# A fused attention and mixture-of-experts kernel: the rank matmuls one step later, the zero-and-one rows in blocks, and two moves in the first expert passes

## The chip, the cores and the metric

The kernel runs on one core of a Trainium2 chip. The metric is the device time of one execution in microseconds. Every kernel is run several times; the profile is one further execution that was recorded instruction by instruction, so its own time need not be the median of the others.

## The reference: what is computed

Attention over 8 batches x 8 heads, 576 positions, 64 wide, where each position sees itself and the 63 before it. Its output, as 4608 rows of 512, goes to a top-1 mixture of 8 experts:

```
mask = (rel >= 0) & (rel < 64)                # rel = query position - key position
attn = softmax(where(mask, q k^T / 8, -1e9))
x = (attn v), as 4608 rows x 512
logits = x @ w_gate                           # 512 x 8
e = argmax(logits); g = softmax(logits)[e]
out[row] = g * (relu(x[row] @ w1[e]) @ w2[e]) # w1 512 x 1024, w2 1024 x 512
```

All in float32, within a tolerance that the kernel keeps by splitting each float32 factor into a rounded part and its remainder (hi and lo) and adding three products.

## The kernel before, in words

**Attention steps.** The rows are cut into 36 tiles of 128. The main loop (L781) is a software pipeline of 43 steps; step i works on several tiles at once: the scores of tile i (TensorE, L368), their masking and maximum (VectorE: L379, L385, L387), the exponentials of tile i-1 (ScalarE, L395), the copy `tsb` of the transposed probabilities of tile i-2 (ScalarE, L404) and their masked halves `pm` (GpSimd, L411, two instructions), the product with the values for tile i-3 (TensorE, L425), its normalisation `xrow` (VectorE, L431 to L435), and, for tile i-4, the transpose of the finished rows (L442) and a copy (ScalarE, L449). The finished rows go to a table `xs` in memory.

**Routing.** Logits are made for two tiles at a time in two steps (L487 and L488, then L469 and L472). The tiles form four rounds of 8, 6, 12 and 10 (`ROUNDS`). When a round's logits are complete, `route` puts eight pieces s1 to s8 into the queue `slow`, and step by step they are taken out. Pieces s1 to s3 (VectorE) find the expert of each token as a 0/1 row `oh`; s4 (TensorE, L521 and L523, then a ScalarE copy `rks`, L525) counts each token's rank among those of its expert; s5 to s8 (VectorE, a little GpSimd) turn ranks into positions. s4 is marked: it is run at the start of a step, the others at a step's end, three per step (`RATE[0]`). Then the queue `puts` is emptied, three entries per step (`RATE[1]`; four from step 36 on): `put(t)` (L570) writes one 128x128 block `hot_row[:, t]` that has a one where a token's position equals the column. After rounds 1 and 2 two more entries follow: `early_parts` (L579, L583, L586: small products `here` and `said`) and one that books for the next three steps the matmuls that make a small table of row numbers (`early_table`, L593, read at L598 to L606), and two gathers (`early_rows`, L170) that fetch the rows of two experts from `xs` into `xg`. The gather for expert 0 fills `xg[0]` with two instructions, which lines 805 and 806 turn (L181, copied by L183 and L184 to `xeh` and `xel`) in steps 27 and 28.

**First passes.** From step 29 on, four early passes (one per expert 0 to 3, 256 rows each, `first_passes`) are woven between the pieces of the attention steps, and go on after the loop. A pass has eight slices j: 12 matmuls with w1 (L286), relu (ScalarE `hh` L292, VectorE `hl` L293), and the matmuls with w2 of the slice before (L250). Each slice of weights is split by ScalarE (`whi`, L224, or L228 ahead of time) and VectorE (`wlo`, L221). After the slices j = 4 and 5 of a pass, the two blocks of rows of the next early pass are turned. `split_ahead` keeps one slice split ahead inside the loop; behind the loop a slice is split where `expert` asks for it (L277). There, between the pieces of the passes, `plan` (L649) computes on VectorE which blocks the later passes take; its pieces are taken one every third piece of a pass. `table(0, NMA)` (L593, 36 matmuls) reads out the row numbers of all later passes.

**Order.** Inside the loop and the early passes the program order is written by hand; every engine takes its instructions in that order, whatever is ready. PSUM banks are shared: `t_b` holds the transposed probabilities and, from step 29, the transposed rows and the turned rows; the scores have two banks, from step 29 only one.

Of the kernel before, what the change touches and what calls it, by code (L numbers as in the profile page):

```python
# [24 lines left out]
P = 128  # L25
# [35 lines left out]
LOADW = 14  # L61
RATE = (3, 3)
AHEAD = 2
# [49 lines left out]
def window_attention_then_top1_moe(ctx: ExitStack, tc: tile.TileContext, qkv, wall, wg, cst, out):  # L113
# [376 lines left out]
    def route(nt, lgs, t0, rnd):  # L490
# [61 lines left out]
        def s8():  # L552
# [6 lines left out]
            nc.vector.tensor_tensor(out=val[:, ts_, 3], in0=v["g1"], in1=val[:, ts_, 2], op=ALU.subtract)  # L559
            for t in range(nt):  # L560
                puts.append(lambda t=t: put(t))
            if rnd in SNAP:
                e0, rows = SNAP[rnd], t0 + nt
                puts.append(lambda: early_parts(e0, rows))
                puts.append(lambda: begin.extend(
                    (rs_["step"] + 1 + k, f) for k, f in enumerate([lambda: early_table(e0, rows)] + [
                        lambda e=e: early_rows(e, rows) for e in range(e0, e0 + 2)])))

        def put(t):
            nc.vector.tensor_scalar(out=hot_row[:, t0 + t], in0=rowb, scalar1=v["lo"][:, t:t + 1], scalar2=None,  # L570
                                    op0=ALU.is_equal)

        slow.extend((f is s4, f) for f in (s1, s2, s3, s4, s5, s6, s7, s8))

# [33 lines left out]
    def early_parts(e, nt):  # L608
        for b in parts(rt, cc("first")[:, 2 * e:2 * e + 4], nt, 4):
            keep["early"] = b  # L610

# [142 lines left out]
    def first_passes():  # L754
        for e in range(EARLY):
            ms = range(2 * e, 2 * e + 2)
            for j in expert(xe[e % 2], cols(eidx, ms), cols(egate, ms), ew[e],
                            lambda: ew[e + 1] if e + 1 < EARLY else wts[0]):
                if e + 1 < EARLY and j == 3:
                    ew[e + 1] = Weights(e + 1)  # L760
                if e + 1 < EARLY and j in (4, 5):
                    turn(xg[(e + 1) % 3], j - 4, xe[(e + 1) % 2])
                    if (e, j) == (EARLY - 2, 5):
                        keep["turned"] = True
                yield e, j
# [14 lines left out]
    with tc.manual_schedule():  # L780
        for i in range(NS + LAST):  # L781
# [12 lines left out]
            if slow and slow[0][0]:  # L794
                slow.popleft()[1]()
            while begin and begin[0][0] <= i:
# [63 lines left out]
        rest = steps()  # L860
        for e, j in early:
            next(rest, None)
            if e == EARLY - 1 and j == NJ - 3:
# [66 lines left out]
```

## Time and profile before

| | |
|---|---|
| three runs | 686.11, 689.41, 689.62 us (median 689.41) |
| the profiled execution | 684.16 us, span of its instructions 682.4 us |
| TensorE busy | 625.0 us, 92% of the span |
| VectorE busy | 413.8 us, 61% |
| ScalarE busy | 359.5 us, 53% |
| GpSimd busy | 194.9 us, 29% |
| mean granted TensorE clock | 0.981 of full speed |

A busy share is an average over the stages. PE is TensorE, PEld its weight loads, DVE VectorE, ACT ScalarE, POOL GpSimd. In a timeline each row is a start, a duration, the engine, the line of the kernel, the operation, what it writes and reads, how many equal instructions were merged, and in brackets how long the engine had stood idle and what ended the wait.

### The profile page before, as it was taken

Reading aid. Unit: us, or ns where it says so; the run is one execution under the profiler, and the core shown is the slowest. Engines: PE = TensorE matmul, PEld = TensorE weight load, DVE = VectorE, ACT = ScalarE, POOL = GpSimd, SP = SyncE. Lnnn points to the kernel's source line nnn. Section 1 sums busy time; section 2 is a strip of 40 time slices with the busy share of each in tenths; the row PEclk is TensorE's granted clock in tenths of the full one; section 3 lists DMA queues with packets and bytes.
Section 4 is the critical chain, followed back from the end, with each engine's and each line's share of the span. In section 5 each row is a group of like instructions: output and inputs, shape, how many; then the busy total and the mean of one; then the engine's idle time right before and its main releaser. Section 6 shows DMA issues by size and latency. Waiting matters only on the chain.

```text
span 682.4 us, 17092 instructions
## 1 busy us (share of the span) xinstructions
PE 625.0 (92%) x7002; PEld 551.8 (81%) x7002; DVE 413.8 (61%) x805; ACT 359.5 (53%) x760; POOL 194.9 (29%) x171
## 2 busy tenths in 40 slices
PE   5797987887789888999999999999999999999995
PEld 4686776766677677889999999999999999999994
DVE  4775978664865896464444655565655556555651
ACT  4564764654453343553535555555556565555551
POOL 4564654632334113330112122121213121110011
PEclk9998986999999999999999999999999999999998
DMA  8997874772324554864354666666567566555620
GB/s 296 332 286 254 281 250 167 268 239 97 109 95 175 198 172 142 326 207 144 142 168 172 229 220 224 216 222 233 166 238 231 208 222 228 202 206 186 217 93 32
DMA packets 34247, 138.14 MB, mean 202 GB/s; under 512 B 4844, under 2 KB 5996, under 8 KB 24432
## 3 DMA queue, kind: packets, MB, share of 16 engines
q1 hardware_dynamic: 27760, 118.08, 50.2%
q0 software_dynamic: 6400, 18.88, 7.9%
q8 instruction: 57, 0.93, 0.5%
q14 instruction: 30, 0.25, 0.1%
HBM read 119.11 MB, written 19.92 MB: 204 GB/s over the span
## 4 chain that ended last, share of the span: by engine, by line
PE 73%; DVE 13%; issue 6%; ACT 4%; POOL 2%; DMA 1%; POOLq 0%; DVEq 0%; ACTq 0%
PE m_b L286 16%; PE x_b L250 14%; PE s_b L250 14%; PE t_b L286 13%; PE x_b L425 5%; PE s_b L368 3%; ACT pf L395 2%; PE s_b L181 2%; DVE wlo L221 2%; DVE xrow L435 1%; PE x_b L487 1%; POOL pm L411 1%; DVE s_b L385 1%; DMA ring<-qkv 1%; DVE s_b L379 1%
## 5 line engine op out<-in xcount | busy, mean ns | idle before, releaser
L221 DVE TENSOR_TENSOR wlo<-raw,whi 128x1024 fp32r<-128x1024 f32 (+1 forms) x158 | 187.2, 1185 | 167.1 <-ACT whi L224 163.0
L224 ACT CAST whi<-raw 128x1024 fp32r<-128x1024 f32 (+1 forms) x147 | 149.1, 1015 | 102.1 <-PE s_b L250 51.3
L411 POOL TENSOR_TENSOR pm<-tsb,cs 128x512 f32<-128x512 f32 x72 | 91.2, 1288 | 93.5 <-ACT tsb L404 85.2
L258 POOL DMA_INDIRECT out<-ys,idx_sb x32 | 40.9, 1277 | 182.9 <-ACT ys L257 178.0
L170 POOL DMA_INDIRECT xg<-xs,idx_sb x32 | 34.3, 1072 | 156.5 <-PE s_b L181 139.1
L286 PE MATMUL t_b<-xh,whi 128*128 128x256 f32 (+1 forms) x240 | 70.6, 294 | 0.0
L286 PE MATMUL m_b<-xh,whi 128*128 128x256 f32 (+1 forms) x240 | 70.5, 294 | 0.0
L250 PE MATMUL s_b<-whi,hh 128*128 128x512 f32 x176 | 70.4, 400 | 0.0
L286 PE MATMUL m_b<-xh,wlo 128*128 128x256 f32 (+1 forms) x240 | 69.9, 291 | 0.0
L250 PE MATMUL s_b<-whi,hl 128*128 128x512 f32 x176 | 69.3, 394 | 0.6 <-DVE hl L293 0.6
L286 PE MATMUL m_b<-xl,whi 128*128 128x256 f32 (+1 forms) x240 | 69.7, 290 | 0.2 <-DVE xl L184 0.2
L395 ACT ACTIVATE pf<-s_b,mxs 128x64 f32<-128x64 f32 x288 | 62.9, 336 | 12.9 <-PE s_b L368 6.7
L286 PE MATMUL t_b<-xh,wlo 128*128 128x256 f32 (+1 forms) x240 | 69.6, 290 | 0.0
L250 PE MATMUL s_b<-wlo,hh 128*128 128x512 f32 x176 | 69.5, 395 | 0.0
L286 PE MATMUL t_b<-xl,whi 128*128 128x256 f32 (+1 forms) x240 | 69.2, 288 | 0.0
L292 ACT ACTIVATE hh<-m_b 128x256 fp32r<-128x256 f32 (+1 forms) x82 | 32.5, 396 | 59.6 <-PE m_b L286 59.5
L425 PE MATMUL x_b<-ring,pm 64*64 64x65 f32 x2176 | 49.0, 233 | 14.4 <-issue 4.8
L425 PEld LDWEIGHTS x_b<-ring,pm 64*64 64x64 f32 x2176 | 43.8, 145 | 19.9 <-issue 15.4
L250 PE MATMUL x_b<-wlo,hh 128*128 128x512 f32 x144 | 56.7, 394 | 0.0
L250 PE MATMUL x_b<-whi,hl 128*128 128x512 f32 x144 | 56.5, 393 | 0.0
L250 PE MATMUL x_b<-whi,hh 128*128 128x512 f32 x144 | 56.5, 392 | 0.0
L293 DVE SCALAR_TENSOR_TENSOR hl<-m_b,hh 128x256 fp32r<-128x256 f32 (+1 forms) x82 | 35.4, 432 | 25.0 <-ACT hh L292 24.9
(178 smaller groups left out, 1280.0 us busy)
## 6 DMA issues: line engine op xcount, KB each, us to landing
raw<-wall SPq DMA_DIRECT2D x76, 1024.0 KB, 4.9
ring<-qkv SPq DMA_DIRECT2D x66, 386.0 KB, 4.6
xs<-xrow SPq DMA_DIRECT2D x36, 256.0 KB, 2.9
ring<-qkv SPq DMA_DIRECT2D x4, 256.0 KB, 5.6
ring<-qkv SPq DMA_DIRECT2D x4, 130.0 KB, 5.4
ring<-qkv SPq DMA_DIRECT2D x1, 512.0 KB, 3.8
xg<-xs,idx_sb POOLq DMA_INDIRECT x32, 4.1
out<-ys,idx_sb POOLq DMA_INDIRECT x32, 2.8
```

The source lines that it names most:

```text
L170: nc.gpsimd.indirect_dma_start(out=t[:, u], out_offset=None, in_=xs[0:rows], in_offset=bass.IndirectOffsetOnAxis(ap=ix, axis=0), bounds_ch ...
L221: nc.vector.tensor_tensor(out=lo[:, s], in0=raw[:, s], in1=hi[:, s], op=ALU.subtract)
L224: nc.scalar.copy(out=hi[:, s], in_=raw[:, s])
L250: nc.tensor.matmul(y, lhsT=x[:, us], rhs=w[:, C:], start=(j == 0 and m == 0), stop=(j == NJ - 1 and m == 2))
L258: ins = nc.gpsimd.indirect_dma_start(out=out, out_offset=bass.IndirectOffsetOnAxis(ap=ix, axis=0), in_=ys, in_offset=None, bounds_check=N ...
L286: nc.tensor.matmul(hp[:, 0:w], lhsT=a[:, ks], rhs=x[:, kk, 0:w], start=(m == 0), stop=(m == 11))
L292: nc.scalar.activation(out=hh[:, 0:w], in_=hp[:, 0:w], func=AF.Relu)
L293: nc.vector.scalar_tensor_tensor(out=hl[:, 0:w], in0=hp[:, 0:w], scalar=0.0, in1=hh[:, 0:w], op0=ALU.max, op1=ALU.subtract)
L368: nc.tensor.matmul(sp[cols, a, g], lhsT=q_r[rows, r, g], rhs=k_r[rows, r - 1:r + 1, g], start=True, stop=True)
L395: nc.scalar.activation(out=pf[:, g, a], in_=sp[:, a, g, 0], func=AF.Exp, bias=mx[:, h:h + 1], scale=SCALE)
L411: nc.gpsimd.tensor_tensor(out=pm[i], in0=t.rearrange("p (g q) -> p g q", g=NG), op=ALU.mult, in1=cc("mask")[:, i * P:(i + 1) * P].unsqueez ...
L425: nc.tensor.matmul(x_b[cols, a, g * V1:(g + 1) * V1], lhsT=pm[i][rows, g, cols], rhs=v_r[rows, c % RING - i, g], start=(i == 0), stop=(i = ...
```

## The change

Six edits. In `route`, an empty entry that is marked like s4 is put before s4 in all rounds but the last, so that s4 runs a step later. `put` writes up to four blocks with one instruction that compares two broadcast operands, and its queue entries become blocks of four tiles; two entries per step are taken instead of three. `early_parts` becomes three entries of two instructions each. In the early passes the two blocks of the next pass are turned after the slices j = 5 and 6. Behind the loop, `split_ahead` is called, and the VectorE half of the split queued, after each slice, ahead of the next piece of `plan`.

```
-RATE = (3, 3)
+RATE = (3, 2)
+PUT = 4
...
-            for t in range(nt):
-                puts.append(lambda t=t: put(t))
+            for t in range(0, nt, PUT):
+                puts.append(lambda t=t: put(t, min(t + PUT, nt)))
...
-                puts.append(lambda: early_parts(e0, rows))
+                puts.extend(early_parts(e0, rows))
...
-        def put(t):
-            nc.vector.tensor_scalar(out=hot_row[:, t0 + t], in0=rowb, scalar1=v["lo"][:, t:t + 1], scalar2=None,
-                                    op0=ALU.is_equal)
-
-        slow.extend((f is s4, f) for f in (s1, s2, s3, s4, s5, s6, s7, s8))
+        def put(a, b):
+            nc.vector.tensor_tensor(out=hot_row[:, t0 + a:t0 + b], in0=rowb.unsqueeze(1).to_broadcast([P, b - a, P]),
+                                    in1=v["lo"][:, a:b].unsqueeze(2).to_broadcast([P, b - a, P]), op=ALU.is_equal)
+
+
+        again = (None,) if rnd + 1 < len(ROUNDS) else ()
+        slow.extend((f in (None, s4), f) for f in (s1, s2, s3, *again, s4, s5, s6, s7, s8))
...
     def early_parts(e, nt):
-        for b in parts(rt, cc("first")[:, 2 * e:2 * e + 4], nt, 4):
-            keep["early"] = b
+        made = []
+
+        def some(k):
+            if not made:
+                made.append(parts(rt, cc("first")[:, 2 * e:2 * e + 4], nt, 4))
+            for _ in range(k):
+                keep["early"] = next(made[0])
+
+        return [lambda k=k: some(k) for k in (2, 2, 2)]
...
-                if e + 1 < EARLY and j in (4, 5):
-                    turn(xg[(e + 1) % 3], j - 4, xe[(e + 1) % 2])
-                    if (e, j) == (EARLY - 2, 5):
+                if e + 1 < EARLY and j in (5, 6):
+                    turn(xg[(e + 1) % 3], j - 5, xe[(e + 1) % 2])
+                    if (e, j) == (EARLY - 2, 6):
                         keep["turned"] = True
...
             if slow and slow[0][0]:
-                slow.popleft()[1]()
+                f = slow.popleft()[1]
+                if f:
+                    f()
...
         for e, j in early:
+            if j is not None:
+                split_ahead()
+                while lows:
+                    lows.popleft()()
             next(rest, None)
```

What this does to the order is shown at three places. First TensorE at round 1 (6 tiles), where step 19 ends and step 20 begins, before the change: transposes of step 19 (L442, L400), the first of the rank matmuls, then the scores and values of step 20.

```order
L469 MATMUL x_b<-cs_81,lgT 128x128 x2
L442 MATMUL m_b<-cs_81,xrow 128x128 x4
L400 MATMUL t_b<-cs_81,pf 128x128 x4
L521 LDWEIGHTS tri
L521 MATMUL x_b<-oh,tri 128x56
...
L523 MATMUL x_b<-oh,ones 128x8
L368 MATMUL s_b_75<-ring 64x128 x16
L425 MATMUL x_b<-ring,pm_1746 64x65 x4
```

The same place after the change (line numbers one higher); L369 is the scores, L426 the values, L488 the logits, L443 and L401 the transposes of step 20.

```order
L443 MATMUL m_b<-cs_81,xrow 128x128 x4
L401 MATMUL t_b<-cs_81,pf 128x128 x4
L369 MATMUL s_b_75<-ring 64x128 x16
...
L488 MATMUL x_b<-xT,wg_sb 32x128 x8
L443 MATMUL m_b<-cs_81,xrow 128x128 x4
L401 MATMUL t_b<-cs_81,pf 128x128 x4
L522 LDWEIGHTS tri
L522 MATMUL x_b<-oh,tri 128x56
...
L524 MATMUL x_b<-oh,ones 128x8
L369 MATMUL s_b_76<-ring 64x128 x16
```

The scores, values, logits and transposes of step 20 now stand between the transposes of step 19 and the rank matmuls, which stand before the scores of step 21.

Second VectorE after round 1, where the blocks `hot_row` are written, before: the last of s8 (`val`), three blocks, a quarter of a weight split, and the start of the next step's masking.

```order
L558 CAST val<-g_2043 128x6
L559 TENSOR_TENSOR val<-g_2043,val 128x6
L570 TENSOR_SCALAR hot_row<-rowb,lo 128x128 x3
L221 TENSOR_TENSOR wlo<-raw,whi 128x256
L378 MEMSET s_b_75 64x8x64
...
L488 COPY lgT<-x_b 128x256
L570 TENSOR_SCALAR hot_row<-rowb,lo 128x128 x3
```

After:

```order
L559 CAST val<-g_2135 128x6
L560 TENSOR_TENSOR val<-g_2135,val 128x6
L571 TENSOR_TENSOR hot_row<-rowb,lo 128x512
L571 TENSOR_TENSOR hot_row<-rowb,lo 128x256
L222 TENSOR_TENSOR wlo<-raw,whi 128x256
L380 COPY_PREDICATED s_b_76<-fold,s_b_76 128x8x64
```

All six tiles of the round are written in one step by two instructions; the step is step 22, one later than the first three blocks before.

Third GpSimd, where the gathers of experts 0 and 1 (`xg_97` is `xg[0]`, `xg_98` is `xg[1]`) stand between the `pm` pairs of the steps, before:

```order
L411 TENSOR_TENSOR pm_2288<-tsb,cs_81 128x512
L411 TENSOR_TENSOR pm_2289<-tsb,cs_81 128x512
L170 DMA xg_97<-xs,eidx 128x512 x2
L411 TENSOR_TENSOR pm_2391<-tsb,cs_81 128x512
L411 TENSOR_TENSOR pm_2392<-tsb,cs_81 128x512
L170 DMA xg_98<-xs,eidx 128x512 x2
```

After:

```order
L412 TENSOR_TENSOR pm_2253<-tsb,cs_81 128x512
L412 TENSOR_TENSOR pm_2254<-tsb,cs_81 128x512
L412 TENSOR_TENSOR pm_2375<-tsb,cs_81 128x512
L412 TENSOR_TENSOR pm_2376<-tsb,cs_81 128x512
L171 DMA xg_97<-xs,eidx 128x512 x2
L412 TENSOR_TENSOR pm_2464<-tsb,cs_81 128x512
L412 TENSOR_TENSOR pm_2465<-tsb,cs_81 128x512
L171 DMA xg_98<-xs,eidx 128x512 x2
```

Both gathers stand one `pm` pair, that is one step, later (steps 26 and 27 instead of 25 and 26), while the turns of `xg[0]` stay in steps 27 and 28.

## Rows read from the trace of the kernel before

**Rows 1.** The page: the span in 40 equal slices, TensorE's busy tenths and its granted clock.

```profile
PE   5797987887789888999999999999999999999995
...
PEclk9998986999999999999999999999999999999998
```

**Rows 2.** Busy time in four stretches: start and end, length, then for each engine its busy time and instructions, the granted clock, the share of the DMA engines and GB/s.

```profile
60.00:140.00 80.00, 65.82 (x1716) 56.79 (x1718) 61.77 (x183) 47.77 (x174) 44.29 (x41) 0.89 0.71 243
140.00:212.00 72.00, 61.56 (x1185) 50.76 (x1178) 46.16 (x122) 33.55 (x96) 25.16 (x21) 0.98 0.36 124
...
234.00:300.00 66.00, 59.35 (x391) 52.36 (x390) 46.91 (x89) 31.45 (x48) 16.77 (x14) 1.00 0.56 198
300.00:656.00 356.00, 355.82 (x2216) 322.68 (x2215) 197.73 (x257) 195.59 (x289) 64.28 (x54) 1.00 0.59 203
```

**Rows 3.** TensorE's timeline at the rank matmuls of round 0 (first row) and round 1, with the scores and values behind them and the scores of the step after.

```profile
62.34 0.19 PE L521 MATMUL x_b<-oh,tri 128*128 128x72 bf16 x1 [1.76 <-DVE oh L516]
...
89.70 0.19 PE L521 MATMUL x_b<-oh,tri 128*128 128x56 bf16 x1 [2.17 <-DVE oh L516]
...
89.95 1.90 PE L368 MATMUL s_b<-ring 64*64 64x128 f32 x32
91.61 1.98 PE L425 MATMUL x_b<-ring,pm 64*64 64x65 f32 x64
...
95.11 1.10 PE L368 MATMUL s_b<-ring 64*64 64x128 f32 x32
```

**Rows 4.** VectorE's timeline in the same two steps: the instructions before which it stood idle.

```profile
64.67 0.70 DVE L379 COPY_PREDICATED s_b<-fold,s_b 128x512 f32<-128x512 int32 x1 [2.38 <-ACT pf L395]
...
67.00 0.17 DVE L431 TENSOR_SCALAR den<-x_b 128x8 f32<-128x8 f32 x1 [0.70 <-PE x_b L487]
...
91.90 0.70 DVE L379 COPY_PREDICATED s_b<-fold,s_b 128x512 f32<-128x512 int32 x1 [1.91 <-PE s_b L368]
...
94.30 0.17 DVE L431 TENSOR_SCALAR den<-x_b 128x8 f32<-128x8 f32 x1 [0.77 <-PE x_b L487]
```

**Rows 5.** The timeline of VectorE (s8's first instruction in round 0, then two groups of three blocks in round 1) and of GpSimd (the `pm` pair beside the first of these groups).

```profile
72.09 0.69 DVE L553 SCALAR_TENSOR_TENSOR lo<-mid,pf 128x8 f32<-128x8 f32 x1
...
101.03 2.73 DVE L570 TENSOR_SCALAR hot_row<-rowb,lo 128x128 bf16<-128x128 bf16 x3
...
107.70 0.57 DVE L570 TENSOR_SCALAR hot_row<-rowb,lo 128x128 bf16<-128x128 bf16 x3
...
101.19 2.52 POOL L411 TENSOR_TENSOR pm<-tsb,cs 128x512 f32<-128x512 f32 x2 [0.80 <-ACT tsb L404]
```

**Rows 6.** Groups of equal instructions on VectorE: busy time, mean ns of one, idle time before them.

```profile
L435 DVE TENSOR_TENSOR xrow<-x_b,rs 128x512 f32<-128x512 f32 x36 | 24.9, 691 | 1.4 <-DVE rs L433 0.2
L570 DVE TENSOR_SCALAR hot_row<-rowb,lo 128x128 bf16<-128x128 bf16 x36 | 10.4, 348 | 0.0
...
L293 DVE SCALAR_TENSOR_TENSOR hl<-m_b,hh 128x256 fp32r<-128x256 f32 x74 | 31.0, 418 | 22.8 <-ACT hh L292 22.7
```

**Rows 7.** TensorE's timeline in steps 23 and 24: the values of step 23 and the scores of step 24.

```profile
107.92 2.01 PE L425 MATMUL x_b<-ring,pm 64*64 64x65 f32 x64 [3.80 <-DVE lgT L488]
...
113.27 1.98 PE L368 MATMUL s_b<-ring 64*64 64x128 f32 x32
```

**Rows 8.** The gathers: GpSimd's timeline (first gather of expert 0, the `pm` pair of step 25, first gather of expert 1), TensorE's (scores of step 25, then the two turns of `xg[0]`), and the time from issue to landing of the four gathers of line 170 between 100 and 135 us.

```profile
117.19 1.25 POOL L170 DMA_INDIRECT xg<-xs,eidx  x1 [0.17 <-issue]
...
121.49 2.68 POOL L411 TENSOR_TENSOR pm<-tsb,cs 128x512 f32<-128x512 f32 x2 [1.74 <-ACT tsb L404]
124.32 1.04 POOL L170 DMA_INDIRECT xg<-xs,eidx  x1 [0.15 <-issue]
...
118.72 1.10 PE L368 MATMUL s_b<-ring 64*64 64x128 f32 x32
...
127.16 0.66 PE L181 MATMUL m_b<-cs,xg 128*128 128x128 f32 x4 [0.24 <-ACT xT L449]
...
131.83 0.66 PE L181 MATMUL m_b<-cs,xg 128*128 128x128 f32 x4 [0.24 <-ACT xT L449]
...
DMA to landing us min/median/max: 3.5/5.8/6.5
```

**Rows 9.** TensorE's timeline at the rank matmuls of round 2 (step 32) and the scores behind them.

```profile
160.82 0.21 PE L521 MATMUL x_b<-oh,tri 128*128 128x104 bf16 x1 [1.28 <-DVE oh L516]
...
163.34 1.10 PE L368 MATMUL s_b<-ring 64*64 64x128 f32 x32 [1.52 <-ACT pf L395]
```

**Rows 10.** TensorE's timeline in steps 34 and 35: a matmul that waits for split weights, and the row transposes behind the two turns of expert 1's rows.

```profile
182.89 0.38 PE L286 MATMUL m_b<-xeh,wlo 128*128 128x256 f32 x1 [0.79 <-DVE wlo L221]
185.03 0.66 PE L442 MATMUL t_b<-cs,xrow 128*128 128x128 f32 x4 [1.75 <-DVE xel L184]
...
194.68 0.66 PE L442 MATMUL t_b<-cs,xrow 128*128 128x128 f32 x4 [1.40 <-DVE xel L184]
```

**Rows 11.** Behind the loop: TensorE's timeline at a wait for split weights and at the table, and VectorE's at a split after two other pieces of work.

```profile
235.35 0.39 PE L286 MATMUL m_b<-xeh,wlo 128*128 128x256 f32 x1 [0.73 <-DVE wlo L221]
...
261.94 2.65 PE L593 MATMUL s_b<-said,hot_row 128*128 128x160 bf16 x36 [1.40 <-DVE xel L184]
...
246.92 1.35 DVE L583 TENSOR_TENSOR said<-here,val 128x1152 bf16<-128x1152 bf16 x1
249.23 1.23 DVE L221 TENSOR_TENSOR wlo<-raw,whi 128x1024 fp32r<-128x1024 f32 x1 [0.97 <-ACT whi L224]
```

## The prediction

> **What bounds the kernel now.** I read the slices of the page first: TensorE is busy nine tenths or more from the eighteenth slice on, and all the thin slices lie ahead of it [rows 1]. The table by stretches says it closer: from 300 to 656 us TensorE works 355.82 of 356.00 us at full clock, so nothing that the change does can shorten that part; a gain must come from the first 300 us [rows 2]. Between 60 and 140 us neither TensorE (65.82 of 80) nor VectorE (61.77 of 80) is full, and the granted clock is 0.89. There the timelines of both engines count, since each waits for the other in turn. The waits that this change touches are these. At the rank matmuls TensorE stands 1.76 and 2.17 us for `oh`, and right behind the second of these waits the scores take 1.90 and the values 1.98 us, where the scores of the next step take 1.10: the lower of the two clock levels, 1.2 GHz, follows an idle TensorE [rows 3]. VectorE, which made `oh` and has little else until scores arrive, stands 2.38 and 0.70 us in the one step, 1.91 and 0.77 in the other [rows 4]. In step 23 TensorE waits 3.80 us for a small copy that stands behind the blocks on VectorE, and the scores of step 24 are at 1.98 again [rows 7].
>
> All sums are made against the profiled execution, 684.16 us. The median of the runs shown is 689.41, 5.25 above it; I put the sum on the median's basis at the end.
>
> **Term 1, ranks a step later, rounds 0 and 1.** The new empty entry takes the place of s4, so the scores, values and transposes of a whole step stand between the transposes and the rank matmuls. TensorE reaches the ranks some 3 us of its own work later (scores 1.10 and values about as much, transposes 0.66 a set [rows 8, 10]), more than the 1.76 and 2.17 that it waited; the wait for `oh` goes, and with it the low clock behind it (1.90 against 1.10, 0.8 for the scores alone). TensorE's gain is not the kernel's: VectorE is nearer the bound, and it can win only what it stood idle, 2.38 + 0.70 + 1.91 + 0.77 = 5.76 [rows 3, 4]. I take the two large waits whole, 4.29, and a third of the small ones, 0.5: **-4.8**. The ends: -5.8 (all of it), and -2.2 (half of the large ones, the rest met again as a wait for the scores). The pieces s5 to s8 and the blocks of the round come one step later too; in these rounds only the table of term 3 needs them.
>
> **Term 2, blocks.** 36 instructions of 348 ns on average, 10.4 us with their waits, become eight of 128x512 and two of 128x256 [rows 6]. No such comparison is in the trace. The nearest rows are `xrow`, 691 ns for 128x512 from two operands, and `hl`, 418 ns for 128x256: 8 x 0.69 + 2 x 0.42 = 6.4 us. The old blocks without a wait took 0.57 / 3 = 0.19 each, 36 x 0.19 = 6.8. The work is equal; what counts is the wait. Three blocks took 2.73 us where they met a `pm` pair (101.03 to 103.76, the pair 101.19 to 103.71), and 0.57 where they did not: 2.16 lost, and behind it the 3.80 of TensorE and the low clock [rows 5, 7]. The six blocks of round 1 now come in step 22 as two instructions. If the meeting goes: -2.16, and 0.88 for scores at 1.10 instead of 1.98, -3.0. If a pair of 128x512 blocks of round 0 now waits out a pair of 2.52: +2.5. Where the blocks fall against `pm` the order doesn't tell; a smaller number of instructions meets it less often, but is held longer when it does. I take two fifths of the better end, **-1.2**.
>
> The Trainium skill ("SBUF — State Buffer", section "SBUF: two separate sides") bears on this: GpSimd and VectorE share a port pair under an exclusive lock, and a VectorE instruction that reads two operands from SBUF needs it as well as one in a fast mode does; the one that starts first holds the other off. The trace agrees: the 2.73 us of the old blocks ended 0.05 us after the pair did, and a two-operand instruction of s8 took 0.69 us for 128x8 elements [rows 5]. By that rule the new form is no cure, and its result is the first rival below.
>
> **Term 3, gathers a step later, turns where they were.** The table moves from step 24 to 25 and the gather of expert 0 behind the `pm` pair of step 25, where expert 1's stands now: 124.32, that is 5.6 us behind the scores of that step (118.72). Landing takes 3.5 to 6.5, 5.8 at the median, so the rows of the first block are there 9.1 to 12.1 us behind those scores. TensorE comes to the first turn 8.4 us behind them today (127.16), and perhaps 7 with steps that lost their waits [rows 8]. At the median that is a wait of 5.6 + 5.8 - 8.4 = 3.0 that was not there, in front of step 27's scores; behind it on TensorE stand those scores, and VectorE waits for them. I take three quarters, since part of it lies beside VectorE's backlog: **+2.2**. Ends: 0 (landing in 3.5 us into a step like today's leaves 0.7, which VectorE's own work covers) and +4.
>
> **Term 4, steps 32 to 36.** In round 2 the wait of 1.28 for `oh` goes by the same means; the one of 1.52 for `pf` behind it stays, since `rks` still stands ahead of the exponentials on ScalarE [rows 9]. The turns of expert 1's rows move from steps 34 and 35 to 35 and 36. With the first go 0.79 of waiting for `wlo` and 1.75 for `t_b`, which the turned rows held; step 35 keeps its 1.40, and step 36 gets such a wait anew, about 1.5 [rows 10]. -1.28 - 0.79 - 1.75 + 1.5 = -2.3; for a longer wait behind `rks` I give back 0.5: **-1.8**. Ends 0 and -3.8 (nothing new in step 36).
>
> **Term 5, behind the loop.** Splitting ahead takes the wait for `wlo` (0.73), and the turned rows no longer stand in front of the 36 matmuls of the table (1.40): 2.13 [rows 11]. Against it: `said` (1.35 us) fills VectorE's time today while ScalarE makes `whi`, and `wlo` then waits only 0.97. Now `wlo` stands ahead of it in the queue, and VectorE would wait up to 1.35 more while the plan's pieces come later. I give back two thirds, 0.9: **-1.2**. Ends -2.1 and, with twice that loss, +0.6. The parts of the early table in three entries move about 1.5 us of work to a neighbouring step and I set them at nothing: VectorE does the same instructions in the same two steps; in a step that is full they would cost at most that, which lies inside the ends of term 1. The plan itself ends early enough for the chain from 300 us, whose TensorE never waits.
>
> The sum: -4.8 - 1.2 + 2.2 - 1.8 - 1.2 = **-6.8**, 677.4 for a profile, and with 5.25 on top **682.6 us** for a median. All ends together: -5.8 - 3.0 + 0 - 3.8 - 2.1 = -14.7 and -2.2 + 2.5 + 4 + 0 + 0.6 = +4.9.
>
> **Rivals.** First, the blocks meet `pm` again. For it speaks that all their operands lie in SBUF, as those of the 2.73 us did; against it, that they are ten and no longer 36. Term 2 becomes +2.5, and with the low clock behind the wait, 0.9, +3.4: 4.6 worse than forecast, **687.2**.
>
> Second, slower: the gather of expert 0 lands late. Place: the first turn, step 27. If steps are shorter and the landing as slow as the slowest today, TensorE waits 5.6 + 6.5 - 7 = 5.1 us or, with the DMA engines 0.71 busy in that stretch [rows 2], longer. That is over the 3.80 behind which scores ran at 1.2 GHz [rows 7]; the scores and values of two steps at 0.9 more each are nearly 4 on top. Without term 3 the sum is -9.0, so the kernel is slower from a wait of about 5 us on: at 7 it costs 11, **691.4**. Against it: landings of 3.5 are in the same rows, and a late TensorE gets part back from the backlog of VectorE.
>
> Third, the waits only move: `oh` comes no earlier, and VectorE, asked for scores, masks and route pieces in the same number of instructions, is the bound of these steps whatever TensorE waits for. Terms 1 and 4 go to nothing: -6.8 + 6.6 = -0.2, **689.2**. For it: 61.77 busy of 80 is only the mean of full and empty steps [rows 2]; against it, that VectorE itself stands idle in just these steps [rows 4].
>
> **How the numbers follow.** The forecast gets 0.55, the meeting of blocks and `pm` 0.22, the late gather 0.13, the moved waits 0.10. A measurement of this kernel tells about 0.5% from no change, that is outside 686.0 to 692.9. Of the forecast 0.50 lies below 686.0 and 0.05 above; the first rival gives 0.07 faster, 0.13 the same, 0.02 slower; the second 0.04 the same and 0.09 slower; the third 0.01, 0.06 and 0.03. Together 0.58 faster, 0.28 the same, 0.14 slower. The range runs from 676, just inside the better ends of the terms (674.7), to 690.5, which takes in the first and third rival and the smaller part of the second; the forecast's own is 678 to 687.
>
> **What would show it.** Term 1: no wait for `oh` at the rank matmuls, scores behind them at 1.10, and steps 14 and 20 no longer than their neighbours. Term 2: block instructions near 0.69 and 0.42 us; one of 2 us or more, ended by a `pm` pair, is the first rival. Term 3: the wait in front of the first turn of `xg[0]`; 3 us bears me out, 5 and a clock of 0.5 behind it is the second rival. Term 4: no wait at the ranks of round 2, the 1.75 gone from step 34 and one of its kind in step 36. Term 5: the table with no wait for `xel`, VectorE idle before `wlo` near 247. I am wrong if TensorE's steady stretch begins no earlier than now although these waits are gone: then what set the early time was something that I don't see in these rows.

## The result, and the profile after

The changed kernel is slower: median 692.47 us over 20 runs (688.17 to 696.04) against 687.85 of the kernel before (20 runs, the three shown earlier among them). The ratio is 1.0081, with a 95% interval of 1.0061 to 1.0100; forecast were 682.6 us and 676 to 690.5, so the time lies above the range. Executions more than 1.5% above the fastest of their kernel, such as two of the 20 before at 1202 and 1519 us, are left out of every ratio, which is therefore not the quotient of these medians. Its profiled execution has a span of 688.8 us, 6.4 more than that of before.

The page of the changed kernel, TensorE's busy tenths and its granted clock in 40 slices:

```profile
PE   6797887788869888999999999999999999999995
...
PEclk9999999999969999999999999999999999999998
```

Before, the clock was at 8, 8 and 6 in the fourth, sixth and seventh slices [rows 1]. Now these are at 9, and a 6 stands in the twelfth, where TensorE's busy tenth is 6 too: from 189 to 207 us. The table by stretches (start and end, length, busy time and instructions of PE, PEld, DVE, ACT and POOL, granted clock, share of the DMA engines, GB/s) says the same:

```profile
60.00:140.00 80.00, 62.52 (x1711) 53.03 (x1713) 63.34 (x172) 47.80 (x174) 45.38 (x41) 0.96 0.71 243
140.00:212.00 72.00, 58.53 (x1087) 48.56 (x1079) 45.59 (x108) 32.27 (x93) 27.24 (x23) 0.91 0.37 127
...
234.00:300.00 66.00, 59.31 (x381) 51.93 (x380) 47.77 (x99) 28.53 (x45) 15.46 (x13) 0.97 0.53 190
300.00:656.00 356.00, 355.18 (x2210) 321.59 (x2209) 199.28 (x258) 196.17 (x289) 63.97 (x54) 1.00 0.60 204
```

In the stretch from 60 to 140 us the clock is 0.96 where it was 0.89; in that from 140 to 212 us it is 0.91 where it was 0.98, and 98 fewer matmuls were done there (1087 against 1185 [rows 2]).

TensorE's timeline at the rank matmuls of rounds 0, 1 and 2 answers to [rows 3] and [rows 9]:

```profile
65.50 0.19 PE L522 MATMUL x_b<-oh,tri 128*128 128x72 bf16 x1 [0.54 <-DVE lgT L489]
...
95.19 0.19 PE L522 MATMUL x_b<-oh,tri 128*128 128x56 bf16 x1 [0.56 <-DVE lgT L489]
...
95.43 1.10 PE L369 MATMUL s_b<-ring 64*64 64x128 f32 x32
...
167.20 0.21 PE L522 MATMUL x_b<-oh,tri 128*128 128x104 bf16 x1 [1.28 <-DVE lgT L489]
```

The waits of 1.76 and 2.17 us for `oh` are 0.54 and 0.56, now for `lgT`, and the scores behind the second take 1.10 and no longer 1.90. In round 2 the wait is as long as before; only its releaser changed.

What came in their place stands at the blocks. Round 0, the end of step 16: the two block instructions on VectorE, the `pm` pair beside them on GpSimd, and TensorE's values of step 18 behind them:

```profile
75.94 2.37 DVE L571 TENSOR_TENSOR hot_row<-rowb,lo 128x512 bf16<-128x512 bf16 x2
...
76.34 3.09 POOL L412 TENSOR_TENSOR pm<-tsb,cs 128x512 f32<-128x512 f32 x2 [1.04 <-ACT tsb L405]
...
81.15 1.39 PE L426 MATMUL x_b<-ring,pm 64*64 64x65 f32 x64 [2.48 <-DVE lgs L473]
```

Round 2, steps 34 and 35, where the largest loss begins: blocks, `pm` pair, the weight split, `xel` of the turn, and the transposes behind it:

```profile
182.42 2.38 DVE L571 TENSOR_TENSOR hot_row<-rowb,lo 128x512 bf16<-128x512 bf16 x2
...
182.86 3.08 POOL L412 TENSOR_TENSOR pm<-tsb,cs 128x512 f32<-128x512 f32 x2 [1.14 <-ACT tsb L405]
...
184.72 2.29 DVE L222 TENSOR_TENSOR wlo<-raw,whi 128x1024 fp32r<-128x1024 f32 x1
...
188.80 0.68 DVE L185 TENSOR_TENSOR xel<-t_b,xeh 128x512 fp32r<-128x512 f32 x1
...
189.54 1.11 PE L443 MATMUL t_b<-cs,xrow 128*128 128x128 f32 x4 [3.29 <-DVE xel L185]
```

The blocks take 2.38 us instead of 1.29 (old_turns_no_split, below), the split 2.29 instead of 1.22, so `xel` comes late. The turned rows hold the bank `t_b` until then; TensorE waits 3.29 us, and its transposes then take 1.11 where 0.66 is usual: the lower level, 1.2 GHz, with a granted clock of 0.52 from 189.5 to 195.5 us. Two steps later VectorE meets a pair again, behind the turn that now stands in step 36:

```profile
199.02 0.66 PE L182 MATMUL t_b<-cs,xg 128*128 128x128 f32 x4 [0.68 <-ACT xT L450]
201.08 0.66 PE L401 MATMUL t_b<-cs,pf 128*128 128x128 f32 x4 [1.05 <-DVE xel L185]
...
202.31 1.68 DVE L586 TENSOR_TENSOR said<-here,val 128x104 bf16<-128x104 bf16 x3
202.48 2.63 POOL L412 TENSOR_TENSOR pm<-tsb,cs 128x512 f32<-128x512 f32 x2 [6.39 <-ACT tsb L405]
203.91 1.25 DVE L589 TENSOR_SCALAR said<-here,cs 128x104 bf16<-128x104 bf16 x1
...
205.21 0.85 PE L596 MATMUL x_b<-said,hot_row 128*128 128x20 bf16 x26 [3.47 <-DVE said L589]
```

`said` and the `pm` pair begin within 0.2 us of each other; four instructions that take 0.85 us in old_turns_no_split need 2.9, and the early table, which stands in the next step, waits 3.47 for them. Not all of that is the meeting: VectorE had stood idle 5.16 us in front of the `xel` of this turn.

To place the loss I set two marks in every profile, at instructions that all kernels have: the scores of step 34, and the one wait of 0.45 or 0.46 us for `wlo` in the first slices behind the loop. The stretch between them, before, then changed (same columns):

```profile
178.32:222.05 43.73, 38.23 (x621) 31.35 (x621) 28.64 (x74) 19.60 (x43) 17.73 (x14) 0.96 0.34 120
```

```profile
176.45:227.37 50.92, 40.69 (x620) 33.79 (x620) 31.28 (x72) 19.79 (x43) 19.60 (x17) 0.87 0.31 113
```

The same matmuls (621 and 620 on record) take 7.19 us longer. Up to step 34 the changed kernel was 1.87 ahead in these two profiles; from the second mark to TensorE's last wait for `hl` ahead of the steady stretch it took 78.67 instead of 77.38 us, 1.3 more. These three parts make the 6.6 by which the steady stretch begins later.

### The profile page after: what moved, and what is told of

It is laid out like the page before. It is cut to its first block, busy times and chain, and to the rows that moved or that the text cites. A ratio compares the mean times of both kernels' runs of the same rounds, so it can differ in the third digit from the quotient of the medians.

```text
span 688.8 us, 17072 instructions
## 1 busy us (share of the span) xinstructions
PE 626.8 (91%) x7002; PEld 552.9 (80%) x7002; DVE 415.4 (60%) x779; ACT 359.8 (52%) x760; POOL 195.2 (28%) x171
## 4 chain that ended last, share of the span: by engine, by line
PE 70%; DVE 14%; issue 7%; ACT 4%; POOL 2%; DMA 1%; POOLq 0%; DVEq 0%; ACTq 0%
PE m_b L287 16%; PE s_b L251 14%; PE x_b L251 13%; PE t_b L287 13%; PE x_b L426 4%; PE s_b L369 3%; DVE wlo L222 2%; ACT pf L396 2%; PE s_b L182 2%; POOL pm L412 1%; PE x_b L488 1%; DVE s_b L386 1%; DVE xrow L436 1%; DVE s_b L380 1%; DVE hot_row L571 1%
## 5 line engine op out<-in xcount | busy, mean ns | idle before, releaser
L222 DVE TENSOR_TENSOR wlo<-raw,whi 128x1024 fp32r<-128x1024 f32 (+1 forms) x158 | 189.4, 1200 | 170.4 <-ACT whi L225 152.0
L225 ACT CAST whi<-raw 128x1024 fp32r<-128x1024 f32 (+1 forms) x129 | 130.2, 1010 | 99.9 <-PE s_b L251 51.4
L426 PE MATMUL x_b<-ring,pm 64*64 64x65 f32 x2176 | 48.0, 224 | 18.2 <-issue 8.1
L426 PEld LDWEIGHTS x_b<-ring,pm 64*64 64x64 f32 x2176 | 41.9, 136 | 24.1 <-issue 17.1
```

The costliest lines, as they stand in the source:

```text
L222: nc.vector.tensor_tensor(out=lo[:, s], in0=raw[:, s], in1=hi[:, s], op=ALU.subtract)
L225: nc.scalar.copy(out=hi[:, s], in_=raw[:, s])
L426: nc.tensor.matmul(x_b[cols, a, g * V1:(g + 1) * V1], lhsT=pm[i][rows, g, cols], rhs=v_r[rows, c % RING - i, g], start=(i == 0), stop=(i = ...
```

## The experiments

Three theories. **A**: the blocks in their new form meet the `pm` pairs. **B**: what a round feeds comes a step late. **C**: the turns or the splits lose the time. All ratios are to the kernel before, on the same chip; the interval is 95%. Each group of four kernels had a chip of its own, so ratios of different groups are compared by way of the kernel before.

**single_blocks**: the blocks in their old form.

```
-RATE = (3, 2)
+RATE = (3, 3)
...
-            nc.vector.tensor_tensor(out=hot_row[:, t0 + a:t0 + b], in0=rowb.unsqueeze(1).to_broadcast([P, b - a, P]),
...
+            nc.vector.tensor_scalar(out=hot_row[:, t0 + t], in0=rowb, scalar1=v["lo"][:, t:t + 1], scalar2=None,
...
```

> The changed kernel with the blocks as before: 128x128 each, one tensor operand and a scalar per partition, three queue entries per step. All else as changed. Theory A (the two-operand blocks meet the pm pairs; VectorE stands for them, frees the PSUM banks late, and TensorE idles 2.5 to 3.5 us three times and falls to 1.2 GHz): the losses go, ratio to before 0.995 (0.991 to 1.000), and the waits of 2.48 and 3.29 us on TensorE in steps 18 and 35 are under 1.8. Rival B (ranks a step later make everything that hangs on them late: the gather at step 27, the small products for the table of step 37): ratio stays at 1.005 to 1.010 and the waits at the turn (1.70 us) and at the table (3.47 us) stay. Rival C (the turns a slice later and the split ahead behind the loop lose the time): ratio 1.006 to 1.010.

Measured: 0.9981 (0.9952 to 1.0010). In theory A's range, if in its upper part, and out of B's and C's. The waits in steps 18 and 35 are 0.70 and 1.40; that at the table is 0.86, though the one at the turn is longer, 4.18. VectorE's blocks and split and GpSimd's pair in step 34:

```profile
182.44 0.57 DVE L571 TENSOR_SCALAR hot_row<-rowb,lo 128x128 bf16<-128x128 bf16 x3
182.87 3.65 POOL L412 TENSOR_TENSOR pm<-tsb,cs 128x512 f32<-128x512 f32 x2 [1.13 <-ACT tsb L405]
182.93 1.22 DVE L222 TENSOR_TENSOR wlo<-raw,whi 128x1024 fp32r<-128x1024 f32 x1
```

The pair begins 0.43 us behind the blocks, as in the changed kernel (0.44), but here the blocks get through in 0.57, the split follows at its usual 1.22, and it is the pair that is held, 3.65 us. The stretch between the marks takes 44.00 us: in step 36 three old blocks still meet a pair and take 2.75.

**ranks_only**: the kernel before with the empty entry alone.

```
+        again = (None,) if rnd + 1 < len(ROUNDS) else ()
+        slow.extend((f in (None, s4), f) for f in (s1, s2, s3, *again, s4, s5, s6, s7, s8))
...
```

> The kernel before with one part of the change alone: the rank matmuls a step later in rounds 0 to 2. Theory A: the waits for oh go and nothing meets worse, ratio 0.995 (0.992 to 0.999). Rival B: the late gather and table cost more than the ranks bring, ratio 1.002 to 1.007. Rival C: no loss here either, 0.993 to 1.000.

Measured: 0.9897 (0.9861 to 0.9933): this part alone gains 1.0%, more than any theory had for it, though the interval reaches into A's and C's ranges. Theory B falls: the later ranks are no loss.

**old_turns_no_split**: turns after slices 4 and 5, no splits ahead behind the loop.

```
-                if e + 1 < EARLY and j in (5, 6):
+                if e + 1 < EARLY and j in (4, 5):
...
-            if j is not None:
-                split_ahead()
-                while lows:
-                    lows.popleft()()
```

> The changed kernel with the turns again after slices 4 and 5 and without the splits ahead behind the loop; ranks and blocks as changed. Theory A: most of the loss stays, ratio 1.004 to 1.010. Rival B: the same, 1.004 to 1.010. Rival C: the loss goes, 0.996 to 1.001.

Measured: 0.9917 (0.9887 to 0.9947). The numbers of A and B were wrong, and C's was too small: without new turns and splits the loss goes, and with the blocks in their new form nearly the whole gain of the ranks is there. Step 34 of this kernel:

```profile
183.95 1.29 DVE L571 TENSOR_TENSOR hot_row<-rowb,lo 128x512 bf16<-128x512 bf16 x2
...
185.15 1.22 DVE L222 TENSOR_TENSOR wlo<-raw,whi 128x1024 fp32r<-128x1024 f32 x1
185.40 3.37 POOL L412 TENSOR_TENSOR pm<-tsb,cs 128x512 f32<-128x512 f32 x2 [2.77 <-ACT tsb L405]
```

The same two blocks take 1.29, because `pm` begins 1.45 us after them and not 0.44 as in the changed kernel. What holds `pm` back is the turn in that step: its rows occupy `t_b`, so the transposes, the ScalarE work behind them (`xT`, the exponentials, the copy `tsb`) and `pm` come later. Counted from the scores of step 34, the turn moves the blocks from 5.97 to 6.57 us, by its own `xel`, and `pm` from 6.41 to 8.02. The stretch between the marks:

```profile
177.38:217.78 40.40, 36.80 (x620) 30.21 (x620) 29.22 (x72) 19.73 (x43) 19.78 (x17) 1.00 0.41 141
```

Full clock, 10.5 us less than the changed kernel.

**no_rank_delay**: the changed kernel without the empty entry.

```
-        again = (None,) if rnd + 1 < len(ROUNDS) else ()
-        slow.extend((f in (None, s4), f) for f in (s1, s2, s3, *again, s4, s5, s6, s7, s8))
+        slow.extend((f is s4, f) for f in (s1, s2, s3, s4, s5, s6, s7, s8))
```

> The changed kernel without the empty entry: the rank matmuls, and all that follows from them, a step earlier, as before; blocks, parts, turns and splits as changed. Theory A: the blocks still meet pm pairs, ratio 1.003 to 1.012, with block pairs of 2 us and more on VectorE. Rival B: the loss goes, ratio at most 1.001. Rival C: 1.004 to 1.010.

Measured: 1.0044 (1.0009 to 1.0079). Blocks, turns and splits still lose time without the delay, as A and C said; B's bound of 1.001 is just inside the interval's lower end.

Four more tell turns, splits and the delay in round 1 apart. **ranks_new_turns** is ranks_only with the new turns:

```
-                if e + 1 < EARLY and j in (4, 5):
+                if e + 1 < EARLY and j in (5, 6):
...
```

> The kernel before with ranks a step later and, on top, the turns after slices 5 and 6; blocks, parts and splits as before. ranks_only gave 0.9897. Theory C1 (the turn a slice later falls on the step in which VectorE has s8 and the blocks of round 2 in front of xel, and costs by itself): 0.993 to 0.998, TensorE's waits in steps 35 to 37 some 3 us more than in ranks_only. Theory C2 (turns cost only where the blocks stand for a pm pair in the same step): 0.988 to 0.992.

Measured: 0.9988 (0.9954 to 1.0022), 0.0091 above ranks_only and just above C1's range: the turns cost even with single blocks. In steps 34 and 35 the blocks take 0.57 us and no wait of TensorE is over 1.40; the loss is in step 36:

```profile
197.17 2.93 DVE L570 TENSOR_SCALAR hot_row<-rowb,lo 128x128 bf16<-128x128 bf16 x4
...
197.34 2.55 POOL L411 TENSOR_TENSOR pm<-tsb,cs 128x512 f32<-128x512 f32 x2 [4.52 <-ACT tsb L404]
...
204.27 0.83 PE L594 MATMUL x_b<-said,hot_row 128*128 128x20 bf16 x26 [3.31 <-DVE said L587]
```

Here it is four old blocks (0.73 us in ranks_only) that end 0.2 us behind the pair, and `said`, behind the last blocks a step later, is late for the table.

**ranks_split** is ranks_only with the splits ahead added behind the loop:

```
+            if j is not None:
+                split_ahead()
+                while lows:
+                    lows.popleft()()
```

> The kernel before with ranks a step later and the splits ahead behind the loop; blocks, parts and turns as before. If the splits lose time (theory C3): 0.993 or more, from the last ranks (round 3) to the last wait for hl at least 1.5 us longer than in ranks_only. If they do nothing, as the equal stretch of 78 us in the four kernels seen so far says: 0.988 to 0.992. My forecast on record had them gain 1.2 us: 0.988.

Measured: 0.9946 (0.9914 to 0.9977), 0.0049 above ranks_only, with intervals that overlap. The stretch that the splits are in, from the second mark to the last wait for `hl`, takes 78.54 us with them and 78.46 without: no gain, and none of the loss that C3 had there. That they cost a few tenths of a per cent elsewhere is not excluded.

**ranks_0_and_2** has the delay in rounds 0 and 2 only (shown against ranks_only):

```
-        again = (None,) if rnd + 1 < len(ROUNDS) else ()
+        again = (None,) if rnd in (0, 2) else ()
```

> The kernel before with the ranks a step later in rounds 0 and 2 only; round 1, with its table and its gathers, as before. If the delay in round 1 pays (the wait of 2.17 us for oh, and the blocks moved off the pm pair) more than the later gather costs: 0.992 to 0.997, above ranks_only. If the later gather costs more: 0.985 to 0.989, under ranks_only.

Measured: 0.9913 (0.9881 to 0.9945), not to be told from ranks_only; the value lies between the two branches of that expectation. Whether the delay in round 1 pays or costs stays open within some 0.5%. The profile leans to a cost: it reaches step 34 at 170.28 us, where ranks_only, ranks_split and ranks_new_turns, which differ from it up to there in round 1 alone, take 175.50 to 177.57.

**changed_no_split** is the changed kernel without the splits:

```
-            if j is not None:
-                split_ahead()
-                while lows:
-                    lows.popleft()()
```

> The changed kernel without the splits ahead behind the loop alone; turns stay after slices 5 and 6, blocks as changed. Theory C2 (new turns and blocks together lose the time in steps 34 to 37): 1.005 to 1.010, as the changed kernel, while old_turns_no_split gave 0.9917. Theory C3 (the splits lose it): 0.990 to 0.996.

Measured: 1.0123 (1.0073 to 1.0173), no better than the changed kernel: C2, whose range the interval reaches, not C3. With the new turns, then, the new form of the blocks costs 1.0123 - 0.9988 = 0.0135; with the old turns 0.9917 - 0.9897 = 0.0020, which is not to be told from nothing. In both pairs RATE and the spread parts change along with it.

The last four look at the place itself. **old_turns_expert_1** moves back only the turns of steps 35 and 36:

```
...
+                d = 4 if e == 0 else 5
+                if e + 1 < EARLY and j in (d, d + 1):
+                    turn(xg[(e + 1) % 3], j - d, xe[(e + 1) % 2])
```

> The changed kernel with only the turns of expert 1's rows back after slices 4 and 5 (steps 34 and 35); those of experts 2 and 3, behind the loop, stay after 5 and 6, splits and blocks as changed. Theory P (the loss is made in steps 34 to 37 alone: without a turn in step 34 the pm pair starts 1 us or more earlier and falls on the blocks, and with a turn in step 36 the products said fall on the pm pair of that step): ratio 0.988 to 0.996, as old_turns_no_split, with the blocks of step 34 at 1.3 us and no wait over 1.5 us on TensorE between step 34 and the end of the loop. Rival Q (the turns behind the loop lose it): 1.004 to 1.012.

Measured: 0.9966 (0.9935 to 0.9997), just above theory P's range, which its interval reaches, and clear of Q's. The stretch between the marks is 40.16 us, the blocks take 1.29 again, and no wait in it is over 1.40. Most of the loss is made in these steps: 1.0081 - 0.9966 = 0.0115 by the turns of one expert. The rest is open. This kernel is 0.0049 above old_turns_no_split, as ranks_split is above ranks_only, and both times the slower one has the splits; but the changed kernel, with them, is under changed_no_split.

**table_later** moves the early table of round 2 and its gathers one step later:

```
-                    (rs_["step"] + 1 + k, f) for k, f in enumerate([lambda: early_table(e0, rows)] + [
+                    (rs_["step"] + (2 if rnd == 2 else 1) + k, f) for k, f in enumerate([lambda: early_table(e0, rows)] + [
```

> The changed kernel with the early table of round 2, and its two gathers, one step later (step 38, where it stood before). Turns, blocks and splits as changed. If TensorE's wait of 3.5 us for said at the table, and the low clock behind it, are a loss by themselves: 1.002 to 1.006, 2 to 4 us under the changed kernel, and that wait is gone. If the time is lost anyway to what holds said up on VectorE: 1.007 to 1.011.

Measured: 1.0088 (1.0055 to 1.0121). `said` still meets `pm` (1.71 and 1.27 us), the wait of 3.47 at the table becomes one of 1.80, and the time stays. The profile has 48.43 us between the marks, 2.5 under the changed kernel; the runs don't show that gain. The interval reaches down to the other theory's range, so this one stays unsettled.

**blocks_before_val** has the blocks right behind `lo`:

```
+            for t in range(0, min(nt, 2 * PUT), PUT):
+                put(t, min(t + PUT, nt))
             nc.vector.tensor_copy(out=val[:, ts_, 1], in_=v["g"])
...
```

> The changed kernel with the first two blocks of each round directly behind lo, ahead of the four small val instructions, so 0.8 us earlier. Theory (blocks and pm pair hold each other off through their start times): in step 34 the two blocks end before or just in the first pm instruction, 1.3 to 1.6 us instead of 2.4; the val instructions meet it instead. Ratio 1.002 to 1.008: a part of the loss goes, most stays, since four small instructions are then held. Rival (the blocks are simply long by their form): they stay at 2.1 us or more.

Measured: 1.0136 (1.0087 to 1.0186), no gain at all; the forecast of a part was wrong. Step 34 of it:

```profile
190.78 1.29 DVE L573 TENSOR_TENSOR hot_row<-rowb,lo 128x512 bf16<-128x512 bf16 x2
...
191.83 2.62 POOL L412 TENSOR_TENSOR pm<-tsb,cs 128x512 f32<-128x512 f32 x2 [1.13 <-ACT tsb L405]
192.00 1.27 DVE L559 CAST val<-g 128x12 bf16<-128x12 f32 x1
193.29 1.18 DVE L560 TENSOR_TENSOR g<-g,val 128x12 f32<-128x12 f32 x1
...
198.56 0.66 PE L443 MATMUL t_b<-cs,xrow 128*128 128x128 f32 x4 [3.34 <-DVE xel L185]
```

The blocks get through, as the theory said, but two instructions of 128x12 elements, 0.18 us elsewhere, then take 1.27 and 1.18, one for each half of the pair. The rival, blocks long by their form, falls. The wait for `xel` is 3.34, as it was: here it does not matter what is held, only that something stands there.

**blocks_only** is the kernel before with the blocks of four:

```
-RATE = (3, 3)
+RATE = (3, 2)
+PUT = 4
...
-            for t in range(nt):
-                puts.append(lambda t=t: put(t))
+            for t in range(0, nt, PUT):
+                puts.append(lambda t=t: put(t, min(t + PUT, nt)))
...
```

> The kernel before with the blocks alone (four tiles per instruction, two entries per step); ranks, parts, turns and splits as before. If the blocks cost by themselves: 1.003 to 1.008, some pairs of blocks at 2 us and more. If they cost only together with the new turns, whose missing wait in step 34 brings pm onto them: 0.998 to 1.002.

Measured: 1.0040 (1.0007 to 1.0074). The blocks, with the two entries per step that come with them, cost by themselves, 2.7 us of 684. The dearest row is in round 1 (blocks, `pm`, and the wait of the table, which here stands a step earlier than before):

```profile
102.11 2.10 DVE L571 TENSOR_TENSOR hot_row<-rowb,lo 128x512 bf16<-128x512 bf16 x2
102.28 3.05 POOL L412 TENSOR_TENSOR pm<-tsb,cs 128x512 f32<-128x512 f32 x2 [0.81 <-ACT tsb L405]
...
110.27 0.53 PE L595 MATMUL x_b<-said,hot_row 128*128 128x20 bf16 x14 [6.01 <-DVE said L588]
```

The stretch between the two marks, one profile each, orders the kernels by turns and blocks. The changed kernel and changed_no_split have the same order of instructions there, and are 2.2 us apart:

| kernel | turns of expert 1 in steps | blocks | us between the marks | ratio |
|---|---|---|---|---|
| old_turns_expert_1 | 34, 35 | four | 40.16 | 0.9966 |
| old_turns_no_split | 34, 35 | four | 40.40 | 0.9917 |
| ranks_0_and_2 | 34, 35 | one | 41.34 | 0.9913 |
| ranks_split | 34, 35 | one | 41.34 | 0.9946 |
| ranks_only | 34, 35 | one | 41.35 | 0.9897 |
| before | 34, 35, no delay | one | 43.73 | 1 |
| blocks_only | 34, 35, no delay | four | 45.52 | 1.0040 |
| single_blocks | 35, 36 | one | 44.00 | 0.9981 |
| ranks_new_turns | 35, 36 | one | 45.42 | 0.9988 |
| no_rank_delay | 35, 36, no delay | four | 46.47 | 1.0044 |
| blocks_before_val | 35, 36 | four, early | 48.00 | 1.0136 |
| table_later | 35, 36 | four | 48.43 | 1.0088 |
| changed_no_split | 35, 36 | four | 48.68 | 1.0123 |
| changed | 35, 36 | four | 50.92 | 1.0081 |

ranks_only beats both kernels: 680.02 us where the kernel before took 686.21 on that chip, a ratio of 0.9897.

## Why the prediction was wrong, point by point

**Term 4 failed, and with it the sign.** The step was: "With the first go 0.79 of waiting for `wlo` and 1.75 for `t_b`, which the turned rows held". It took both waits of step 34 as the turn's, and as time that comes back when the turn moves. The runs showed two other things. First, most of these waits was not the turn's. In the kernel before, the blocks ahead of that split and that `xel` met a `pm` pair:

```profile
178.82 2.51 POOL L411 TENSOR_TENSOR pm<-tsb,cs 128x512 f32<-128x512 f32 x2 [3.10 <-ACT tsb L404]
...
180.04 1.66 DVE L570 TENSOR_SCALAR hot_row<-rowb,lo 128x128 bf16<-128x128 bf16 x3
```

The blocks take 1.66 us and not 0.57, the last instruction of s8 ahead of them 1.25 and not 0.19. In ranks_only the turns stay and the blocks come a step later, behind this `xel`; there the wait of 0.79 is gone and that of 1.75 is 0.64:

```profile
182.11 0.66 PE L442 MATMUL t_b<-cs,xrow 128*128 128x128 f32 x4 [0.64 <-DVE xel L184]
```

So the delay brought 1.9 of the 2.54 us, and moving the turn could bring 0.64 at most. Second, the turn of step 34 was the spacer between VectorE's work at the step's end and the `pm` pair. Without it `pm` begins 1.45 - 0.44 = 1.0 us nearer to the blocks and falls on them, and the turn in step 36 puts `said` on the next pair. I forecast -1.8 for steps 32 to 36; between the marks the changed kernel took 7.19 more. For the turns alone the runs gave +0.9% (some 6 us) with the old blocks; with the new ones 1.0123 - 0.9917 = 2.1%, or 0.0115 for those of expert 1. I priced each wait of the turn by what TensorE stood there, and never asked what else had made it long, nor when GpSimd would start once the turn was gone.

**Term 2 failed in sign.** I forecast -1.2; blocks_only gave +2.7. The price of an instruction was right: 0.68 us for 128x512 alone (0.69 forecast), 1.29 for two. The mean in the changed kernel was another:

```profile
L571 DVE TENSOR_TENSOR hot_row<-rowb,lo 128x512 bf16<-128x512 bf16 x8 | 7.4, 956 | 0.0
...
L571 DVE TENSOR_TENSOR hot_row<-rowb,lo 128x256 bf16<-128x256 bf16 x2 | 1.9, 958 | 0.0
```

956 ns and not 690. The first rival came true, and more of it: I let one pair be met, in round 0; in the profile it happened in rounds 0, 1 and 2 (2.37, 2.10 and 2.38 us). I gave it 0.22 as if where the blocks fall were luck. In rounds 1 and 2 it is mostly order: the blocks of round 1 take 2.10 us in seven profiles, those of round 2 2.37 to 2.39 in the three with this order. In round 0 it is luck: with one and the same order they took 2.37 in three profiles and 1.28 in two. The part where the Trainium skill ("SBUF — State Buffer", section "SBUF: two separate sides") spoke against the change was right: by its rule a VectorE instruction that reads two operands from SBUF, or works in a two-port mode, waits for a GpSimd instruction that reads SBUF and started first. The trace agrees for both forms of the blocks: 2.38 us for two new ones, 2.93 for four old ones in ranks_new_turns.

**Term 1 was right in sign; its size is not shown.** The waits for `oh` fell by 1.22 and 1.61 us, to waits for `lgT`. The ranks alone gave -1.0%, some 7 us, where terms 1 and 3 and the 1.28 of term 4 had -4.8 + 2.2 - 1.28 = -3.9 for them. The 1.28 itself did not go; between the marks the delay brought 43.73 - 41.35 = 2.4 us, 1.9 of it the two waits under term 4. Of the rest, part is a meeting that went away and not idle time of VectorE: the first three blocks of round 1, 2.73 us before [rows 5], take 1.66 in ranks_only and 0.57 in ranks_split, ranks_new_turns and ranks_0_and_2.

**Term 3 came, but not by its own cause alone.** The wait in front of the first turn was forecast at 3.0:

```profile
128.55 0.63 PE L182 MATMUL m_b<-cs,xg 128*128 128x128 f32 x4 [1.70 <-DMA xg<-xs,eidx]
```

1.70 here; 1.52, 3.44, 3.45 and 3.52 in the four profiles with the same order up to there (old_turns_no_split, table_later, old_turns_expert_1, changed_no_split). But in ranks_only, ranks_split and ranks_new_turns, where table and gathers are as late, TensorE waits 0.24 there, as before [rows 8]: the wait came only where the new blocks or parts joined the delay; which of them makes it is open. The second rival, 5 us and more, did not come.

**Term 5 was mis-sized.** The wait of 1.40 at the 36 matmuls is gone, as forecast, but the stretch behind the loop is no shorter (78.67 against 77.38, with 75.92 to 78.67 in the fourteen profiles), and ranks_split gained nothing there. Waits for `wlo` only moved.

```profile
236.66 0.39 PE L287 MATMUL t_b<-xeh,wlo 128*128 128x256 f32 x1 [1.84 <-DVE wlo L222]
```

A wait of this kind at 239.67 was 1.25 before, the longest there. The two profiles with the new turns and no splits have the shortest stretch, 75.92 and 76.82: that the turns gain there and the splits take it back is not excluded. The third rival, waits that only move because VectorE bounds the steps, fits here; against it for term 1 stands the gain of the ranks. The parts in three entries, set at nothing, are not cleared: with the turn in step 36 they lie in front of `pm`; without it they cost nothing between the marks (40.40 against 41.35).

## What to carry to other kernels

Work that one engine waits for may be what keeps two others apart. Before it is moved, ask what else makes the wait long, which instruction starts earlier then, and lay its new start beside what the other engine does at that moment. And where an instruction can be held for as long as a neighbour's whole operation, its price is the start time and not its duration: moving the blocks by 0.8 us handed the wait to the next in the queue.

## What the runs showed of the hardware that was not expected

VectorE and GpSimd hold each other in both directions and instruction by instruction. When VectorE is first, its work goes through at its usual time and the pair is stretched: 3.65 and 3.37 us instead of 2.5. When one `pm` instruction gets in between, VectorE waits for its end, even with 128x12 elements (1.27 us), and may pass ahead of the second, which stretches the pair too (3.08). Which of the two gets in first was not settled: with the pair 0.43 and 0.44 us behind the first block, VectorE kept the way in single_blocks and lost it in the changed kernel, whose first block was longer (0.68 against 0.25 us).

Up to step 34 five kernels have the same order of instructions, and their profiles reach it at 176.45 (changed), 177.38, 180.09, 181.69 and 182.19 us: 5.7 apart. The three late ones, old_turns_expert_1 among them, have the long wait at the turn, and the scores of step 33 at 1.98 or 1.99 instead of 1.10:

```profile
129.20 1.09 PE L182 MATMUL m_b<-cs,xg 128*128 128x128 f32 x4 [3.45 <-DMA xg<-xs,eidx]
...
172.54 1.99 PE L369 MATMUL s_b<-ring 64*64 64x128 f32 x32 [1.18 <-ACT pf L396]
```

So a single profile of this stage says nothing about differences under some 5 us. Between the marks the five profiles with the ranks delayed, the old turns of expert 1 and so no long wait agree to 1.2 us (40.16 to 41.35). The changed kernel and changed_no_split, with one order of instructions, do not (50.92 and 48.68): behind waits of 3.29 and 3.27 us the transposes ran at 1.2 GHz in the first (1.11 us) and at 2.4 GHz in the second (0.66). A wait of that length does not settle the clock behind it.
